# An attention and feed-forward block on one core: second batch in plain products, norm weights moved to the eviction, small work moved between engines

## The chip, the cores and the metric

The kernel runs on one core of one Trainium2 chip. The metric is the device time of one execution, in microseconds, from the first to the last instruction with what lies around them. The engines are TensorE (PE, with its weight loads PEld), VectorE (DVE), ScalarE (ACT), GpSimd (POOL) and SyncE (SP), whose queue issues all the transfers. TensorE's granted clock is given as a share of full speed: 1.00 is 2.4 GHz, and 0.50 is the lower of its two levels, 1.2 GHz.

## The reference, cut to what matters

Eight batches of 448 tokens, 12 heads of 64. Attention with normalised queries and keys, then a Fourier mix over tokens and channels, a layer norm, and a feed-forward with double precision weights that the kernel must first convert:

```python
rms = np.sqrt(np.mean(x * x, axis=-1, keepdims=True) + 1e-06)
q_n, k_n = (rmsnorm(q, g_q), rmsnorm(k, g_k))          # x / rms * g
scores = scale * np.matmul(q_n, k_n.transpose(0, 1, 3, 2))
attn = np.exp(scores - np.max(scores, axis=-1, keepdims=True))
x = np.matmul(attn / (attn.sum(axis=-1, keepdims=True) + 1e-09), v)
...
mixed = np.real(np.fft.fft(np.fft.fft(x, axis=1), axis=2))
u = x + mixed
un = (u - u.mean(-1, keepdims=True)) / np.sqrt(u.var(-1, keepdims=True) + 1e-06)
out = u + np.maximum(un @ w_ch1, 0.0) @ w_ch2
```

`g_q` and `g_k` are vectors of 64, one weight for each channel of a head. Every channel of a query meets the same channel of a key, so the kernel multiplies both weights (and the scale, negated) into one vector `gneg` and applies it to the keys alone.

## The kernel before, in words

**Batches and their two halves.** For each batch b there is an auxiliary part, `aux(b)` (attention, Fourier mix, layer norm), and a main part, `ffn(b)` (24 tiles `up` of 18 products, and 36 tiles `down` of 12). `aux(0)` runs first, with 14 steps of `aux(1)` mixed in after its attention. Then `ffn(b)` runs merged with `aux(b + 1)`: both are generators that yield a written cost after every step, and `merge` advances the side work until its cost reaches `RATIO` times that of the main work (0.49; `RATIO_FIRST`, 0.45, for `ffn(0)`). Side steps left over when the main work ends are issued behind it. The kernel asks for a schedule from a timeline model (`schedule_with_timeline_sim=True`), so that the order of the instructions on an engine need not be the written one. `LAG` and `PACE` bind some of them in place.

**Split and plain.** A product in full precision is made either from split operands (high parts and low parts of each value, multiplied in several fast passes, type fp32r) or plainly (type f32). A split needs a ScalarE copy of the high part and a VectorE subtraction for the low part (`sub`); plain operands need one ScalarE copy. `PLAIN_PAIRS` and `PLAIN_SCORES` say which pairs of heads are plain: in batch 0 all six in the value product, and all but the first two in the scores. Every later pair is split. `vhl` holds the split values, `QT` and `KD`/`KL` the transposed queries and keys, `T` and `R` the transposed probabilities, `P` the probabilities, `S` the scores, `mn` their minima.

**The norms.** `norm_pair` squares queries and keys (`sq`, one tile of 112 x 1024 called qkn in the profile), sums (`ss`), takes a power on GpSimd, multiplies the keys by `gneg` (`kf`, called raw<-raw,gneg) and multiplies both by the norms (qkn<-raw,ss, two tiles of 112 x 512). Squares and weight products run on GpSimd but for the first pair; the norm products run on GpSimd for pairs 2 to 8 (counted over batches), else on VectorE.

**The conversion of the weights.** The weights come as doubles. `convert` loads a tile (dblw<-w), and then ScalarE makes two prepared words (lines 702 and 703), VectorE does three bit operations (704, 708, 712), GpSimd adds the low bits (716), ScalarE copies the high part (717) and GpSimd subtracts it for the low part (718). There are 60 tiles: 24 of 768 columns and 36 of 512. 14 are made early, beside `aux(0)`; 46 are made when `ffn(0)` needs them. Later batches read the stored results.

**The Fourier mix.** `fold` makes sums and differences of the transposed attention output on VectorE (first eo<-xT, two additions), `spectral` multiplies by constant matrices (y, ab), `token_tile` adds and normalises, and `ffn_input` transposes for the feed-forward (un, unT). In batch 1 all three folds come after the last pair.

Line 113 of the profile is the wrapper that most VectorE, ScalarE and GpSimd instructions go through, so those are told apart by their tiles. On TensorE, L362 and L365 are scores (plain, split), L439, L443 and L473, L478 value products (plain, split), L898 `up` (h<-unT,w) and L919 `down` (o<-hs,w).

Of the kernel before, what the change touches and what calls it, by code (L numbers as in the profile page):

```python
# [11 lines left out]
F32 = mybir.dt.float32  # L12
# [3 lines left out]
AF = mybir.ActivationFunctionType  # L16
# [29 lines left out]
PLAIN_PAIRS = range(NPAIR)  # L46
PLAIN_SCORES = range(2, NPAIR)
# [42 lines left out]
def spectral_block(ctx, tc, q, k, v, g_q, g_k, w1, w2, d1, d2, out, nb=B):  # L90
# [90 lines left out]
    gneg = cpool.tile([C, D], F32, name="gneg")  # L181
    gtmp = cpool.tile([C, D], F32, name="gtmp")
# [4 lines left out]
    def load_gains():  # L187
        nc.sync.dma_start(gneg, g_q.rearrange("(o d) -> o d", o=1).broadcast_to([C, D]))
        nc.sync.dma_start(gtmp, g_k.rearrange("(o d) -> o d", o=1).broadcast_to([C, D]))
        V.scalar_tensor_tensor(  # L190
            out=gneg, in0=gneg, scalar=-(D**-0.5), in1=gtmp, op0=ALU.mult, op1=ALU.mult
        )
# [49 lines left out]
    def norm_pair(b, p):  # L242
# [5 lines left out]
        (G if nth else V).tensor_tensor(out=sq, in0=flat, in1=flat, op=ALU.mult)  # L248
# [6 lines left out]
        kf = flat[:, 8:]  # L255
        (G if nth else V).tensor_tensor(
            out=kf, in0=kf, in1=gneg[:, None, :].broadcast_to([C, 8, D]), op=ALU.mult
        )
        for i in range(2):
            (G if 2 <= nth < NPAIR * 3 // 2 else V).tensor_tensor(  # L260
                out=qk[:, i].rearrange("t c h d -> t h c d"),
                in0=raw[:, i],
                in1=ss[:, 8 * i : 8 * i + 8]
                .rearrange("t (h c) -> t h c", h=2)[:, :, :, None]
                .broadcast_to([C, 2, NC, D]),
                op=ALU.mult,
            )
# [4 lines left out]
        (G if b < EARLY else V).tensor_tensor(  # L272
# [16 lines left out]
    def transpose_pair(b, p):  # L289
# [8 lines left out]
        if plain_s(b, p):  # L298
            T = []
            for i, tag in enumerate(("QT", "KD")):  # L300
# [8 lines left out]
                A.copy(t, pt[:, :S])  # L309
# [7 lines left out]
        for i in range(2):  # L317
# [7 lines left out]
            if i == 0:  # L325
                A.copy(QT[lo, 0], src[lo])
                A.copy(QT[hi, 1], src[hi])
                sub(QT[hi, 0], src[lo], QT[lo, 0])
                sub(QT[lo, 1], src[hi], QT[hi, 1])
            else:  # L330
                for h, sl in enumerate((lo, hi)):
                    A.copy(KD[sl, h], src[sl])
                    sub(KL[sl, h], src[sl], KD[sl, h])
                A.copy(KD[hi, 0], KD[lo, 0].bitcast(F32))
                A.copy(KD[lo, 1], KD[hi, 1].bitcast(F32))
# [355 lines left out]
    def convert(src, bits, part, name):  # L691
# [26 lines left out]
        behind(nc.gpsimd.tensor_tensor(  # L718
# [287 lines left out]
```

## Time and profile before

| | |
|---|---|
| median of 3 runs | 2237.56 us (2234.73 to 2239.64) |
| the profiled execution, its own time | 2231.58 us |
| its span, first to last instruction | 2229.8 us |
| granted TensorE clock, mean | 0.968 |
| TensorE busy | 2107.0 us (94%) |
| VectorE busy | 1577.0 us (71%) |
| ScalarE busy | 1033.3 us (46%) |
| GpSimd busy | 542.3 us (24%) |

The busy shares are means over stages of very different kinds, and matmul instructions overlap, so a busy TensorE is not one at its peak. Two products that follow each other without a gap are told apart by the distance of their starts.

### The profile page before, as it was taken

To read this page: it belongs to the slowest core of one execution; us is meant where nothing else is said; L and a number is where in the kernel's file an instruction comes from. 1 tells how busy PE (TensorE), PEld (TensorE's weight loads), DVE (VectorE), ACT (ScalarE), POOL (GpSimd) and SP (SyncE) were. 2 spreads that over 40 slices of the span, in tenths; PEclk is the share of its full clock that TensorE was granted. 3 is DMA by queue.
4 is the path that set the end of the run, shared out by engine and by line. 5 is a ranking of instruction groups with operands and counts; after the bars stand their busy time and mean duration, and the time that the engine had idled before them with its cause. 6 is when DMAs were issued, how large, how long until landed. Compare 5 with 4: busy or idle time off the path is not lost.

```text
span 2229.8 us, 31302 instructions
## 1 busy us (share of the span) xinstructions
PE 2107.0 (94%) x11212; PEld 1855.7 (83%) x11212; DVE 1577.0 (71%) x2975; ACT 1033.3 (46%) x2242; POOL 542.3 (24%) x334
## 2 busy tenths in 40 slices
PE   7877988588999999999999999999999999999997
PEld 3336867477999999999999999999999999998997
DVE  6676899887688587866788587866787577763122
ACT  5756766554554355524554355524554355422100
POOL 6753566554121021211121021111211021000000
PEclk8888989799999999999999999999999999999999
DMA  5456555567655675557656675557555674539665
GB/s 171 150 162 203 189 190 193 201 235 244 200 175 174 197 221 167 176 178 224 188 171 183 201 214 165 177 177 230 185 169 179 205 212 159 178 135 289 214 211 137
DMA packets 298237, 425.32 MB, mean 191 GB/s; under 512 B 186545, under 2 KB 224418, under 8 KB 298082
## 3 DMA queue, kind: packets, MB, share of 16 engines
q1 hardware_dynamic: 298082, 423.32, 61.1%
q8 instruction: 89, 1.46, 0.3%
q14 instruction: 66, 0.54, 0.1%
HBM read 363.47 MB, written 65.27 MB: 192 GB/s over the span
## 4 chain that ended last, share of the span: by engine, by line
PE 79%; DVE 8%; DMA 4%; ACT 3%; issue 3%; POOL 2%; SPq 0%; DVEq 0%; POOLq 0%; ACTq 0%
PE h L898 28%; PE o L919 28%; PE S L365 5%; PE av L473 4%; PE pt L461 4%; DMA dblw<-w 2%; PE y L578 1%; PE qk L320 1%; PE av L439 1%; DMA w<-w 1%; POOL magw L716 1%; DVE eo L113 1%; PE oT L864 1%; DVE mn L113 1%; DVE magw L712 1%
## 5 line engine op out<-in xcount | busy, mean ns | idle before, releaser
L919 PE MATMUL o<-hs,w 128*128 128x448 f32 x3456 | 795.2, 372 | 14.9 <-POOL w L718 3.5
L898 PE MATMUL h<-unT,w 128*128 128x448 f32 x3456 | 787.0, 373 | 13.8 <-DVE xT L113 8.1
L898 PEld LDWEIGHTS h<-unT,w 128*128 128x128 f32 x3456 | 646.3, 191 | 68.1 <-issue 8.5
L919 PEld LDWEIGHTS o<-hs,w 128*128 128x128 f32 x3456 | 641.6, 190 | 72.7 <-POOL w L718 5.4
L113 ACT ACTIVATE P<-S,mn 112x448 f32<-112x448 f32 x384 | 243.0, 635 | 226.4 <-DVE mn L113 215.3
L113 DVE TENSOR_REDUCE mn<-S 112x1 f32<-112x448 f32 x384 | 232.3, 617 | 65.0 <-PE S L365 42.3
L113 POOL TENSOR_TENSOR qkn<-raw 112x1024 f32<-112x1024 f32 x47 | 89.7, 1909 | 720.2 <-PE qk L320 476.3
L113 ACT ACTIVATE hs<-h 128x448 fp32r<-128x448 f32 x192 | 104.4, 544 | 305.5 <-PE h L898 304.5
L113 DVE TENSOR_TENSOR acc<-o,acc 128x448 f32<-128x448 f32 x240 | 148.9, 621 | 105.4 <-PE o L919 103.8
L113 DVE SCALAR_TENSOR_TENSOR hs<-h,hs 128x448 fp32r<-128x448 f32 x192 | 119.3, 622 | 134.6 <-ACT hs L113 132.8
L113 ACT CAST T<-pt 128x448 fp32r<-128x448 f32 x252 | 132.7, 532 | 143.9 <-PE pt L461 137.7
L473 PE MATMUL av<-T,vhl 128*128 128x448 f32 x504 | 179.8, 390 | 8.8 <-DVE T L113 5.3
L113 DVE TENSOR_TENSOR T<-pt,T 128x448 fp32r<-128x448 f32 x252 | 154.8, 617 | 28.4 <-ACT T L113 26.8
L113 POOL TENSOR_TENSOR ss<-ss,nhalf 112x16 f32<-112x16 f32 x48 | 143.6, 2992 | 119.9 <-DVE ss L113 112.7
L461 PE MATMUL pt<-ident,P 112*128 112x112 f32 x1008 | 145.8, 264 | 4.5 <-ACT P L113 2.7
L365 PE MATMUL S<-KD,QT 128*112 128x448 f32 x352 | 139.4, 397 | 5.5 <-ACT KD L113 2.4
L461 PEld LDWEIGHTS pt<-ident,P 112*128 112x128 f32 x1008 | 122.6, 143 | 24.7 <-ACT P L113 3.1
L113 POOL TENSOR_TENSOR rstd<-st,nhalf 112x1 f32<-112x1 f32 (+2 forms) x32 | 19.1, 595 | 493.2 <-DVE st L113 493.2
L365 PE MATMUL S<-rounded,QT 128*112 128x448 f32 x352 | 131.8, 376 | 1.2 <-DVE rounded L113 1.2
L113 DVE TENSOR_SCALAR P<-P,sm 112x448 f32<-112x448 f32 x288 | 122.0, 463 | 3.9
L473 PEld LDWEIGHTS av<-T,vhl 128*128 128x128 f32 x504 | 96.1, 192 | 20.0 <-DVE T L113 7.4
L716 POOL TENSOR_TENSOR magw<-magw,dblw 128x512 uint32<-128x512 uint32 (+1 forms) x46 | 71.3, 1551 | 64.1 <-DVE magw L712 41.6
(127 smaller groups left out, 2580.8 us busy)
## 6 DMA issues: line engine op xcount, KB each, us to landing
w<-w SPq DMA_DIRECT2D x288, 512.0 KB, 4.4
w<-w SPq DMA_DIRECT2D x192, 768.0 KB, 4.5
dblw<-w SPq DMA_DIRECT2D x30, 512.0 KB, 4.4
dblw<-w SPq DMA_DIRECT2D x16, 768.0 KB, 4.5
raw<-q SPq DMA_DIRECT2D x96, 112.0 KB, 4.2
raw<-k SPq DMA_DIRECT2D x96, 112.0 KB, 3.8
v<-v SPq DMA_DIRECT2D x96, 96.0 KB, 3.6
u_dram<-u SPq DMA_DIRECT2D x24, 336.0 KB, 3.9
```

The costliest lines, as they stand in the source:

```text
L113: ins = emit(*args, **kwargs)
L320: nc.tensor.transpose(pt[:, c * C : (c + 1) * C], qk[:, i, c].rearrange("t h d -> t (h d)"), ident[:C, :C],)
L365: ins = nc.tensor.matmul(s_, QT[:, h, cs], K[:, h], start=step == 0, stop=step == 1)
L439: nc.tensor.matmul(av[:D, :S], vhl[:, j, h], T, start=j == 0, stop=False)
L461: nc.tensor.transpose(pt[:, c * C : (c + 1) * C], Pc[c][:, 512 * h + j * 128 : 512 * h + (j + 1) * 128], ident[:C, :C],)
L473: nc.tensor.matmul(av[:, :S], lv, T[:, i], start=(j == 0 and i == 0), stop=False)
L578: nc.tensor.matmul(o, src[:, par, t0 : t0 + n], D1[:, ri, par, cols], start=i != 1, stop=i != 0,)
L712: behind(nc.vector.scalar_tensor_tensor(out=bits, in0=high, scalar=0xC0000000, in1=bits, op0=ALU.bitwise_and, op1=ALU.bitwise_or,))
L716: behind(nc.gpsimd.tensor_tensor(out=bits, in0=bits, in1=low, op=ALU.add))
L864: nc.tensor.transpose(op[:n, j * 128 : (j + 1) * 128], accs[b][:, 3 * half + j, t0 : t0 + n], ident,)
L898: pace(nc.tensor.matmul(o, w[:, a, c], unT[c][:, z], start=n == 0, stop=n == 17))
L919: pace(nc.tensor.matmul(o, w[:, a, f], hs[4 * g + f][:, z], start=n == 0, stop=n == 11))
```

## The change

Batch 1 becomes plain as batch 0 is: `PLAIN_PAIRS` and `PLAIN_SCORES` reach to 12 pairs. The weights of the norms are no longer multiplied into the keys; `gains` holds both vectors with one channel a partition (twice, for the two heads), and `gneg` is now a per-partition scale in the eviction of the transposed keys, plain or split. The squares of batches 0 and 1 go from GpSimd (the first from VectorE) to ScalarE; those of later batches stay on GpSimd. The norm products, the low part of the split values and the low part of the converted weights (line 718) all go to VectorE.

```diff
-PLAIN_PAIRS = range(NPAIR)
-PLAIN_SCORES = range(2, NPAIR)
+PLAIN_PAIRS = range(2 * NPAIR)
+PLAIN_SCORES = range(2, 2 * NPAIR)
...
-    gneg = cpool.tile([C, D], F32, name="gneg")
-    gtmp = cpool.tile([C, D], F32, name="gtmp")
+    gains = cpool.tile([128, 2], F32, name="gains")
+    gneg = gains[:, :1]
...
     def load_gains():
-        nc.sync.dma_start(gneg, g_q.rearrange("(o d) -> o d", o=1).broadcast_to([C, D]))
-        nc.sync.dma_start(gtmp, g_k.rearrange("(o d) -> o d", o=1).broadcast_to([C, D]))
+        for i, g in enumerate((g_q, g_k)):
+            for h in range(2):
+                nc.sync.dma_start(
+                    gains[64 * h : 64 * h + 64, i : i + 1],
+                    g.rearrange("(d o) -> d o", o=1),
+                )
         V.scalar_tensor_tensor(
-            out=gneg, in0=gneg, scalar=-(D**-0.5), in1=gtmp, op0=ALU.mult, op1=ALU.mult
+            out=gneg, in0=gneg, scalar=-(D**-0.5), in1=gains[:, 1:], op0=ALU.mult,
+            op1=ALU.mult,
         )
...
-        (G if nth else V).tensor_tensor(out=sq, in0=flat, in1=flat, op=ALU.mult)
+        if b < EARLY:
+            A.activation(sq, flat, AF.Square)
+        else:
+            G.tensor_tensor(out=sq, in0=flat, in1=flat, op=ALU.mult)
...
-        kf = flat[:, 8:]
-        (G if nth else V).tensor_tensor(
-            out=kf, in0=kf, in1=gneg[:, None, :].broadcast_to([C, 8, D]), op=ALU.mult
-        )
         for i in range(2):
-            (G if 2 <= nth < NPAIR * 3 // 2 else V).tensor_tensor(
+            V.tensor_tensor(
                 out=qk[:, i].rearrange("t c h d -> t h c d"),
...
-        (G if b < EARLY else V).tensor_tensor(
+        V.tensor_tensor(
             out=vhl[:, :, 1:3], in0=vt, in1=vhl[:, :, ::3], op=ALU.subtract
         )
...
-                A.copy(t, pt[:, :S])
+                if i == 0:
+                    A.copy(t, pt[:, :S])
+                else:
+                    A.activation(t, pt[:, :S], AF.Copy, scale=gneg)
...
-                    A.copy(KD[sl, h], src[sl])
-                    sub(KL[sl, h], src[sl], KD[sl, h])
+                    A.activation(KD[sl, h], src[sl], AF.Copy, scale=gneg[sl])
+                    V.scalar_tensor_tensor(
+                        out=KL[sl, h], in0=src[sl], scalar=gneg[sl], in1=KD[sl, h],
+                        op0=ALU.mult, op1=ALU.subtract,
+                    )
...
-        behind(nc.gpsimd.tensor_tensor(
+        behind(nc.vector.tensor_tensor(
             out=part[1], in0=value, in1=part[0], op=ALU.subtract
         ))
```

## Rows read from the trace of the kernel before

**Rows 1.** Windows: length, then PE, PEld, DVE, ACT, POOL busy (instructions), TensorE clock, DMA.
```profile
152.00:196.00 44.00, 23.30 (x120) 19.57 (x120) 34.30 (x63) 23.50 (x48) 17.26 (x12) 0.71 0.47 142
196.00:543.00 347.00, 289.45 (x1417) 250.99 (x1418) 293.93 (x456) 211.33 (x412) 205.89 (x131) 0.89 0.64 212
543.00:2229.80 1686.80, 1670.69 (x9221) 1531.42 (x9219) 1147.76 (x2306) 701.67 (x1563) 216.80 (x123) 1.00 0.62 190
```

**Rows 2.** Groups by line, VectorE, 196 to 543 us: busy us, mean ns, idle before.
```profile
L704 DVE TENSOR_SCALAR magw<-magw 128x512 f32<-128x512 f32 x28 | 21.0, 750 | 8.3 <-ACT magw L702 8.2
L708 DVE TENSOR_SCALAR magw<-magw 128x512 uint32<-128x512 uint32 x29 | 23.5, 812 | 0.3
L712 DVE SCALAR_TENSOR_TENSOR magw<-dblw,magw 128x512 uint32<-128x512 uint32 x29 | 27.3, 940 | 0.4
L113 DVE TENSOR_TENSOR T<-pt,T 128x448 fp32r<-128x448 f32 x36 | 21.8, 615 | 1.3 <-ACT T L113 0.9
L113 DVE TENSOR_TENSOR qkn<-raw,ss 112x512 f32<-112x512 f32 x10 | 16.4, 1674 | 0.9 <-POOL ss L113 0.9
```

**Rows 3.** Groups by line, VectorE, 600 to 2000 us.
```profile
L113 DVE TENSOR_TENSOR qkn<-raw,ss 112x512 f32<-112x512 f32 x64 | 41.4, 686 | 3.3 <-POOL ss L113 3.0
L113 DVE TENSOR_TENSOR vhl<-v,vhl 128x512 fp32r<-128x512 f32 x34 | 23.4, 687 | 17.0 <-ACT vhl L113 13.7 <-DMA w<-w 2.9
```

**Rows 4.** Groups by line, GpSimd, 196 to 543 us.
```profile
L718 POOL TENSOR_TENSOR w<-magw,w 128x512 fp32r<-128x512 f32 x30 | 44.0, 1466 | 34.2 <-ACT w L717 34.2
L716 POOL TENSOR_TENSOR magw<-magw,dblw 128x512 uint32<-128x512 uint32 x29 | 38.9, 1340 | 36.9 <-DVE magw L712 26.8 <-ACT u L113 4.1 <-DVE sm L113 2.9
L716 POOL TENSOR_TENSOR magw<-magw,dblw 128x768 uint32<-128x768 uint32 x16 | 31.2, 1949 | 26.5 <-DVE magw L712 14.7 <-issue 8.6 <-ACT hs L113 2.1
L718 POOL TENSOR_TENSOR w<-magw,w 128x768 fp32r<-128x768 f32 x16 | 30.1, 1888 | 12.0 <-ACT w L717 12.0
```

**Rows 5.** Timeline, VectorE: start us, duration us, instruction.
```profile
368.61 0.43 DVE L708 TENSOR_SCALAR magw<-magw 128x512 uint32<-128x512 uint32 x1
369.67 0.68 DVE L712 SCALAR_TENSOR_TENSOR magw<-dblw,magw 128x512 uint32<-128x512 uint32 x1
373.80 3.17 DVE L708 TENSOR_SCALAR magw<-magw 128x512 uint32<-128x512 uint32 x1
```

**Rows 6.** Timeline, GpSimd, the same moment.
```profile
372.74 2.14 POOL L113 TENSOR_TENSOR qkn<-raw 112x1024 f32<-112x1024 f32 x1
375.39 1.28 POOL L718 TENSOR_TENSOR w<-magw,w 128x512 fp32r<-128x512 f32 x1
```

**Rows 7.** Timeline, TensorE: plain products of batch 0, split ones of batch 1.
```profile
93.15 0.96 PE L443 MATMUL av<-R,v 64*64 64x448 f32 x2
94.05 1.76 PE L362 MATMUL S<-KD,QT 64*112 64x448 f32 x8
...
221.03 0.37 PE L365 MATMUL S<-KD,QT 128*112 128x448 f32 x1
221.24 0.36 PE L365 MATMUL S<-rounded,QT 128*112 128x448 f32 x1
```

**Rows 8.** Timeline, VectorE: the first additions of a fold, batches 0 and 1.
```profile
153.43 6.04 DVE L113 TENSOR_TENSOR eo<-xT 128x449 f32<-128x449 f32 x2 [0.26 <-ACT xT L113]
...
449.05 1.15 DVE L113 TENSOR_TENSOR eo<-xT 128x449 f32<-128x449 f32 x2
```

**Rows 9.** Timeline, TensorE: stages' beginnings and ends.
```profile
150.99 0.96 PE L443 MATMUL av<-R,v 64*64 64x448 f32 x2
...
196.09 0.71 PE L898 MATMUL h<-unT,w 128*128 128x448 f32 x1 [0.28 <-DMA w<-w]
...
491.84 0.36 PE L365 MATMUL S<-KD,QT 128*112 128x448 f32 x1
...
541.24 2.18 PE L919 MATMUL o<-hs,w 128*128 128x448 f32 x10
543.26 3.82 PE L898 MATMUL h<-unT,w 128*128 128x448 f32 x18
```

## The prediction, made before the change was run

> **What bounds the kernel now.** I read the windows first: the stretch in which one engine is full, then those before it. After 543 us TensorE is busy 1670.69 of 1686.80 us at a granted clock of 1.00, while VectorE is busy two thirds of that time [rows 1]. Nothing that the change moves between VectorE, ScalarE and GpSimd can shorten that part: it is a block of about 1687 us of matrix work that only starts earlier or later. Everything that the change can win or lose lies ahead of it, in three stretches [rows 1]: the attention of batch 0, its transform and normalisation (152 to 196 us), and the feed-forward of batch 0, which runs beside the attention and the transform of batch 1 and beside 46 weight conversions (196 to 543 us). The third is the long one. TensorE is busy 289.45 of its 347 us, at a granted clock of 0.89, so it has both gaps and slow periods. At the full clock that work would be about 289.45 x 0.89 = 258 us, 74% of the stretch. VectorE is busy 293.93 us, 84.7% of the stretch; GpSimd 205.89 us; ScalarE 211.33 us.
>
> Next I read which VectorE groups fill that stretch. The split of the transposed probabilities (T) is work that only a split batch has [rows 2]. Three bit operations of the conversion (lines 704, 708, 712) and the norm products (qkn) take far longer than the same tiles elsewhere: 750, 812, 940 and 1674 ns [rows 2], against 0.43, 0.43 and 0.68 us in quiet spots [rows 5] and 686 ns after 600 us [rows 3]. The timeline shows why. One instruction of line 708 lasts 3.17 us instead of 0.43 [rows 5]; it starts during a square of 2.14 us on GpSimd and ends at 376.97 us, when GpSimd's narrow subtraction has ended at 376.67 [rows 6]. While GpSimd works on tiles, these VectorE instructions stand still.
>
> The Trainium skill ("SBUF — State Buffer", section "SBUF: two separate sides") says that VectorE and GpSimd share a pair of ports, which one instruction holds for its whole length while the other waits; the 3.17 us agrees with it. The same rule speaks against this change as well: an instruction with two SBUF inputs that moves to VectorE can now be held, and can hold GpSimd's. By the rule alone, if each of the 46 moved subtractions waited for one whole instruction of line 716 (38.9 + 31.2 = 70.1 us in all [rows 4]), the stretch would end at 401 us; the rows, worked out below, give 327. The rule is one more reason behind the last rival.
>
> **The change part by part, in the stretch from 196 to 543 us.**
>
> VectorE loses the splits of batch 1. T: 36 instructions at 615 ns, 21.8 us [rows 2]. By the code there are four more kinds of the same width, which I price at T's mean: 12 splits of the remainders, 12 additions of the two value halves, 8 query remainders (pairs 2 to 5; the first two pairs are done earlier) and 10 key remainders, 42 x 0.615 = 25.8 us. Together 47.6 us.
>
> VectorE gains line 718: 30 tiles of 512 columns and 16 of 768 [rows 4]. Before shows no such instruction on VectorE. The nearest row is the value split of the later batches, a subtraction of the same shape at 687 ns [rows 3]; by columns the wide one is 1.03 us. That gives 30 x 0.687 + 16 x 1.03 = 37.1 us. The dear end is what GpSimd needs for them, 44.0 + 30.1 = 74.1 us [rows 4]. I take the cheap end, since it is a VectorE row. Two norm products come over at 686 ns [rows 3], 1.4 us. Together 38.5 us.
>
> The holding falls. The excess over the quiet durations is 28 x (750 - 430) + 29 x (812 - 430) + 29 x (940 - 680) + 10 x (1674 - 686) ns = 9.0 + 11.1 + 7.5 + 9.9 = 37.5 us [rows 2, 3, 5]. Of GpSimd's 205.9 us [rows 1] line 716 stays with 38.9 + 31.2 = 70.1 us, a third [rows 4]; a few squares and copies stay too, so I take 45% of the holding as left. By the code 144 conversion and norm instructions were exposed to it, and 48 join them (x 1.33): 37.5 x 0.45 x 1.33 = 22.4 us. The relief is 15 us; its ends are 0 and 37.5.
>
> VectorE's sum is then 293.9 - 47.6 + 38.5 - 15 = 269.8 us. At the same share, 84.7%, the stretch would take 318 us: 29 us less by VectorE alone.
>
> ScalarE takes the squares of batches 0 and 1, and loses the second copies of queries, keys and remainders and the value copies. It has 347 - 211 = 136 us free here [rows 1], so I cost it at nothing. The norms' weights now ride in the key eviction: a copy becomes a copy with a scale and a subtraction becomes a scaled one of the same size, nothing. The products with the weights vanish from GpSimd in all batches; after 543 us that is cover under a full TensorE, so nothing there either.
>
> TensorE gains work. In the trace a plain product shows as two instructions (72 for the 36 value products of batch 0 by the code), and such a pair takes 0.90 us, from 93.15 to 94.05 [rows 7]. Split instructions follow each other every 0.21 us [rows 7]. A plain value pair has 8 products, 7.2 us; a split one has 14 instructions, 2.9 us. Six pairs of batch 1 make 6 x 4.3 = 26 us more. The scores come out even: four plain products in 1.7 us [rows 7] make 3.4 us for a pair's eight, and sixteen split ones take 16 x 0.21 = 3.4. TensorE's work in the stretch thus rises from 258 to 284 us at the full clock and passes VectorE's 269.8: VectorE was the tighter engine, TensorE will be. If the tighter one again gets 84.7% of the time, the stretch takes 284 / 0.847 = 335 us; but TensorE can hold 99% where nothing keeps it waiting [rows 1]. Between VectorE's 318 and this 335 I take the middle, 327 us: **20 us less**. The ends are 290 us, if TensorE is kept full, and 381, below.
>
> Start: four small loads of weights are issued where two were. The weights are now needed only at the first key eviction, but the multiplication that joins them still stands in VectorE's queue. The two things point opposite ways, and I take 0.
>
> Up to 196 us: the two first fold additions at 153 us took 6.04 us under GpSimd's work, and 1.15 us in a quieter place [rows 8]. They stand on the chain to the transform, so 4.9 us; with about 1 us for the shorter norm chain (squares and products no longer behind each other on GpSimd) I take 6. The ends are 0, if the moved subtractions come in between, and 15.
>
> **The order of the work.** The merge hands out the side work by its written costs. A plain value pair costs 420 + 2(3 x 1180 + 760) = 9,020 instead of 420 + 2(3 x 800 + 190) = 5,600, so the side work of batch 1 rises from 66,480 to 87,000. The feed-forward of batch 0 hands out 0.45 x 164,160 = 73,900, and 3,540 were handed out before it. So the last 14 steps (9,520), which are the whole transform and normalisation of batch 1, now come behind the last tile of the feed-forward, where before they were done ten steps ahead of its end. What is late next is the first product of the next feed-forward. Before, the first product of batch 1's feed-forward followed the last one of batch 0's at 543 us with no gap [rows 9]: the chain was hidden. Uncovered, it can be seen in batch 0: from the last value product at 151 us to the first product at 196 us [rows 9], 44 us, or 39 without the 4.9 us of holding. VectorE worked 34.3 us in it [rows 1], 29.4 without the holding, which the sum above already counts as 29.4 / 0.847 = 35 us. So the least cost is 4 us, and TensorE's idle time there, 44 - 23.3 = 21 us [rows 1], is the next bound; 44 is the worst. I take 12.
>
> Sum: -20 - 6 + 12 = -14 us. Against the profiled execution (2231.58 us, span 2229.8) that is 2217.6; the median of the runs stands 6.0 us above it, so **2224 us**.
>
> **Rivals.**
>
> *TensorE is kept full.* If conversion tiles and probabilities arrive in time, the stretch shrinks to TensorE's own work, 290 us with a little idle time: -57 - 6 + 12 = -51, 2187 us. For it: VectorE stands 8.3 us ahead of line 704 [rows 2], waiting for a chain that gets shorter. Against it: TensorE idles 58 us there now [rows 1], and no one wait accounts for it.
>
> *The transform is uncovered.* The 14 steps cost their 44 us in full: -20 - 6 + 44 = +18, 2256 us. For it: the written costs. Against it: score products of batch 2 were issued at 491 us [rows 9], ahead of their written place, so the order on the engines is not strictly the written one. It decides from 26 us on.
>
> *VectorE becomes the tighter bound, on the other side.* Line 718 needs the result of a ScalarE copy, for which GpSimd idled 34.2 us ahead of the narrow tiles alone [rows 4]. On GpSimd that idling held up nothing; on VectorE, scores, splits and sums stand behind it. If each moved instruction costs what it did on GpSimd (77.1 us in place of 38.5) and no relief comes, VectorE has 323 us and the stretch takes 381: +34 - 6 + 12 = +40, 2278 us. It decides from the mean price at which the whole change wins nothing: the stretch may then be 341 us, VectorE 288.8, which leaves 57.5 us for 48 instructions, 1.20 us each, against 0.80 in my sum.
>
> **How the numbers follow.** Forecast 0.53, with a range of its own from 2200 to 2240; TensorE kept full 0.17; transform uncovered 0.17; VectorE tighter 0.13. The range from 2178 to 2262 takes in the first three and leaves out the last and the far end of TensorE's. A change of 0.2% (4.5 us) is about what these runs can tell from none. Faster: 0.43 + 0.17 = 0.60; same 0.11, from the forecast's upper end and the mild form of the uncovered transform; slower 0.29, the rest of that form and the last rival.
>
> **What would show it.** After the change, in the stretch up to the second feed-forward: VectorE near 270 us; TensorE's busy time times its clock near 284 us; line 718 near 0.7 and 1.0 us; lines 704 and 708 nearer 0.43; the norm products nearer 0.69; the first fold additions near 1.2 us for two; a low TensorE clock with a gap between the feed-forwards of about 12 us more idle time. The forecast is wrong if the later block is not again about 1687 us, if line 718 is preceded by long VectorE waits, or if that gap is above 35 us.

## The result, and the profile after

The changed kernel takes 2201.66 us (median, 2199.90 to 2206.73) against 2238.60 us of the kernel before on the same chip: a ratio of 0.984, 95% interval 0.983 to 0.986, or 37 us less. The forecast was 14 us less. Its profiled execution lasted 2199.90 us with a span of 2198.1.

The windows of the changed kernel, cut at the first up product of each of the first two feed-forwards, answer to [rows 1] (length, then PE, PEld, DVE, ACT and POOL busy, TensorE clock, DMA):

```profile
0.00:185.00 185.00, 146.38 (x585) 73.66 (x585) 132.35 (x237) 127.51 (x275) 58.48 (x40) 0.87 0.55 167
185.00:504.00 319.00, 300.23 (x1384) 215.28 (x1385) 225.32 (x382) 181.65 (x354) 107.21 (x63) 0.98 0.70 228
504.00:2198.00 1694.00, 1674.88 (x9257) 1536.18 (x9256) 1164.38 (x2346) 723.06 (x1592) 179.15 (x93) 1.00 0.62 190
```

The first stretch is 11 us shorter (185 for 196), the second 28 us (319 for 347), the last block 7 us longer (1694 for 1687): the span falls by 32. The median fell 5 us more, since the profiled execution of before lay 7 us below its median and that of the changed kernel 2. In the second stretch VectorE's share fell from 85% to 71%, and TensorE's clock rose from 0.89 to 0.98. The same stretch in four parts shows what is left:

```profile
185.00:238.00 53.00, 53.00 (x233) 37.89 (x234) 18.26 (x33) 23.98 (x51) 8.77 (x6) 0.96 0.57 197
238.00:424.00 186.00, 179.00 (x810) 120.62 (x809) 145.02 (x233) 120.03 (x236) 73.35 (x43) 1.00 0.74 236
424.00:451.00 27.00, 19.00 (x80) 12.84 (x79) 24.97 (x36) 11.86 (x19) 8.62 (x5) 0.89 0.64 218
451.00:504.00 53.00, 49.24 (x267) 43.94 (x266) 37.07 (x82) 25.78 (x50) 16.47 (x11) 0.96 0.69 239
```

Up to 424 us TensorE is nearly full at the full clock. The one soft spot is 424 to 451 us, where the folds of batch 1 fill VectorE (24.97 of 27 us), TensorE is busy 19 us, and its clock is 0.89.

The VectorE groups of that stretch answer to [rows 2] (busy, mean ns, idle before; the lines are now 714, 718 and 722 for 704, 708 and 712, and 726, 727 and 728 for 716, 717 and 718):

```profile
L728 DVE TENSOR_TENSOR w<-magw,w 128x512 fp32r<-128x512 f32 x30 | 22.7, 759 | 12.1 <-ACT w L727 11.9
L722 DVE SCALAR_TENSOR_TENSOR magw<-dblw,magw 128x512 uint32<-128x512 uint32 x29 | 20.5, 707 | 0.3
L714 DVE TENSOR_SCALAR magw<-magw 128x512 f32<-128x512 f32 x28 | 17.0, 607 | 19.8 <-ACT magw L712 19.8
L728 DVE TENSOR_TENSOR w<-magw,w 128x768 fp32r<-128x768 f32 x16 | 16.7, 1042 | 2.1 <-ACT w L727 2.1
L718 DVE TENSOR_SCALAR magw<-magw 128x512 uint32<-128x512 uint32 x28 | 12.1, 432 | 0.5
L714 DVE TENSOR_SCALAR magw<-magw 128x768 f32<-128x768 f32 x16 | 11.6, 727 | 20.3 <-ACT magw L712 20.3
L113 DVE TENSOR_TENSOR qkn<-raw,ss 112x512 f32<-112x512 f32 x12 | 10.1, 871 | 0.7 <-POOL ss L113 0.7
```

The low part costs 759 and 1042 ns on VectorE, and the bit operations and norm products fell from 750, 812, 940 and 1674 ns [rows 2] to 607, 432, 707 and 871. On GpSimd the addition that stayed (line 726) has a longer mean than in [rows 4], 1540 ns for 1340. Twenty of the 29 still take 1.29 to 1.32 us. Six take 1.51 to 1.55 us and ran beside line 728 or a norm product; three take 2.0, 2.9 and 4.6 us, beside the folds and the transform of batch 1, and the longest of them met no subtraction of line 728.

```profile
L726 POOL TENSOR_TENSOR magw<-magw,dblw 128x512 uint32<-128x512 uint32 x29 | 44.7, 1540 | 91.7 <-DVE magw L722 51.6 <-ACT P L113 11.4 <-DMA v<-v 6.6
```

The timeline of VectorE at batch 0's last fold answers to [rows 8]; the two additions that took 6.04 us take 1.16:

```profile
140.88 1.16 DVE L113 TENSOR_TENSOR eo<-xT 128x449 f32<-128x449 f32 x2
142.07 1.17 DVE L113 TENSOR_TENSOR sd<-eo 128x450 f32<-128x450 f32 x2
```

And the timeline of TensorE where the two feed-forwards meet answers to [rows 9]:

```profile
498.21 2.27 PE L929 MATMUL o<-hs,w 128*128 128x448 f32 x10
500.32 1.15 PE L820 MATMUL un<-ident,un 112*128 112x112 f32 x10
502.29 0.60 PE L820 MATMUL un<-ident,un 112*128 112x112 f32 x4 [0.83 <-ACT un L113]
504.02 0.39 PE L908 MATMUL h<-unT,w 128*128 128x448 f32 x1
```

The last down product ends at 500.5 us, the first up product of batch 1 starts at 504.0, and most of the 3.5 us between is work. The transform of batch 1 ran beside the end of the feed-forward, ahead of its written place, as before.

### The profile page after: what moved, and what is told of

Same layout as the page of the kernel before. It is cut to its first block, busy times and chain, and to the rows that moved or that the text cites. A ratio compares the mean times of both kernels' runs of the same rounds, so it can differ in the third digit from the quotient of the medians.

```text
span 2198.1 us, 31240 instructions
## 1 busy us (share of the span) xinstructions
PE 2121.5 (97%) x11224; PEld 1825.1 (83%) x11224; DVE 1522.0 (69%) x2963; ACT 1032.2 (47%) x2218; POOL 344.8 (16%) x196
## 4 chain that ended last, share of the span: by engine, by line
PE 72%; DMA 2%; DVE 1%; ACT 0%; SPq 0%; issue 0%; DVEq 0%; ACTq 0%
PE h L908 27%; PE o L929 26%; PE S L375 5%; PE av L483 4%; PE pt L471 4%; PE y L588 1%; DMA w<-w 1%; PE qk L327 1%; PE oT L874 1%; PE av L488 1%; PE rem L430 1%; PE x L620 1%; PE ab L661 1%; PE un L820 1%; DMA u_dram<-u 0%; DVE u L113 0%
## 5 line engine op out<-in xcount | busy, mean ns | idle before, releaser
L908 PE MATMUL h<-unT,w 128*128 128x448 f32 x3456 | 773.9, 369 | 6.1 <-DMA w<-w 2.4
L113 POOL TENSOR_TENSOR qkn<-raw 112x1024 f32<-112x1024 f32 x36 | 69.2, 1923 | 692.7 <-PE qk L327 415.8
L113 ACT CAST T<-pt 128x448 fp32r<-128x448 f32 x216 | 113.0, 533 | 102.5 <-PE pt L471 100.9
L483 PE MATMUL av<-T,vhl 128*128 128x448 f32 x432 | 153.4, 383 | 0.0
L113 DVE TENSOR_TENSOR T<-pt,T 128x448 fp32r<-128x448 f32 x216 | 131.6, 618 | 27.5 <-ACT T L113 26.4
L375 PE MATMUL S<-KD,QT 128*112 128x448 f32 x304 | 119.3, 393 | 4.2 <-ACT KD L113 2.8
L471 PE MATMUL pt<-ident,P 112*128 112x112 f32 x864 | 121.4, 259 | 0.0
L471 PEld LDWEIGHTS pt<-ident,P 112*128 112x128 f32 x864 | 102.5, 140 | 15.6
L375 PE MATMUL S<-rounded,QT 128*112 128x448 f32 x304 | 113.4, 374 | 0.0
L483 PEld LDWEIGHTS av<-T,vhl 128*128 128x128 f32 x432 | 80.9, 188 | 7.2
```

What stands on the lines that cost most here:

```text
L113: ins = emit(*args, **kwargs)
L375: ins = nc.tensor.matmul(s_, QT[:, h, cs], K[:, h], start=step == 0, stop=step == 1)
L471: nc.tensor.transpose(pt[:, c * C : (c + 1) * C], Pc[c][:, 512 * h + j * 128 : 512 * h + (j + 1) * 128], ident[:C, :C],)
L483: nc.tensor.matmul(av[:, :S], lv, T[:, i], start=(j == 0 and i == 0), stop=False)
L908: pace(nc.tensor.matmul(o, w[:, a, c], unT[c][:, z], start=n == 0, stop=n == 17))
```

## The experiments

All runs are compared with the kernel before on their own chip. "Transform" is the start of batch 1's first Fourier product (y<-D) in the second stretch, "meeting" the first up product of batch 1; PE and DVE are busy time of the stretch, the clock TensorE's. All times in us, losses against the changed kernel by the medians.

| run | time | ratio [95%] | first up | transform | meeting | PE, clock | DVE | POOL |
|---|---|---|---|---|---|---|---|---|
| before | 2238.6 | 1 | 196 | 457 | 543 | 289, 0.89 | 294 | 206 |
| after | 2201.7 | 0.984 [0.983, 0.986] | 185 | 454 | 504 | 300, 0.98 | 225 | 107 |
| e1 low part on GpSimd | 2220.9 | 0.991 [0.990, 0.993] | 188 | 472 | 525 | 306, 0.95 | 231 | 176 |
| e2 batch 1 split | 2224.1 | 0.993 [0.991, 0.994] | 185 | 449 | 534 | 292, 0.88 | 293 | 110 |
| e3 norms on GpSimd | 2202.3 | 0.983 [0.982, 0.985] | 183 | 463 | 505 | 301, 0.97 | 229 | 115 |
| e4 ratio 0.55 | 2201.2 | 0.983 [0.981, 0.984] | 186 | 468 | 505 | 303, 0.98 | 235 | 103 |
| e8 plain scores, split values | 2213.9 | 0.989 [0.987, 0.991] | 183 | 433 | 522 | 296, 0.93 | 284 | 116 |
| e5 low part alone | 2237.0 | 1.000 [0.998, 1.001] | 196 | 452 | 546 | 293, 0.89 | 299 | 135 |
| e6 plain batch 1 alone | 2235.1 | 0.998 [0.997, 0.999] | 197 | 484 | 539 | 309, 0.95 | 236 | 192 |
| e7 norms alone | 2228.4 | 0.995 [0.993, 0.996] | 192 | 460 | 541 | 287, 0.90 | 291 | 182 |
| e11 weights alone | 2236.2 | 0.999 [0.998, 1.000] | 193 | 450 | 547 | 300, 0.88 | 289 | 195 |
| e9 idle tiles | 2232.3 | 0.998 [0.996, 0.999] | 197 | 508 | 537 | 313, 0.94 | 238 | 121 |
| e10 idle powers | 2216.4 | 0.990 [0.988, 0.992] | 191 | 478 | 517 | 307, 0.96 | 231 | 153 |
| e13 half of the values split | 2209.3 | 0.986 [0.983, 0.989] | 184 | 453 | 520 | 305, 0.94 | 264 | 104 |
| e14 plain values, split scores | 2222.9 | 0.993 [0.991, 0.996] | 184 | 493 | 524 | 303, 0.92 | 246 | 103 |
| e15 half of the scores split | 2218.1 | 0.992 [0.989, 0.995] | 185 | 493 | 520 | 303, 0.93 | 242 | 104 |
| e17 as e14, ratio 0.60 | 2199.2 | 0.983 [0.981, 0.985] | 184 | 420 | 505 | 297, 0.97 | 265 | 109 |
| e18 after, ratio 0.60 | 2200.4 | 0.983 [0.981, 0.985] | 184 | 451 | 503 | 302, 0.97 | 239 | 102 |
| e19 as e1, ratio 0.60 | 2224.8 | 0.993 [0.992, 0.995] | 186 | 464 | 533 | 323, 0.94 | 227 | 181 |
| e20 as e6, ratio 0.60 | 2230.9 | 0.996 [0.994, 0.997] | 196 | 444 | 544 | 321, 0.94 | 241 | 195 |

**One part undone in the changed kernel.** e1 puts the low part back on GpSimd, e2 splits batch 1 again, e3 puts the squares and norm products back on GpSimd, e4 hands the side work out earlier, e8 splits the values alone.

```diff
e1:
-        behind(nc.vector.tensor_tensor(
+        behind(nc.gpsimd.tensor_tensor(
             out=part[1], in0=value, in1=part[0], op=ALU.subtract
e2:
-PLAIN_PAIRS = range(2 * NPAIR)
-PLAIN_SCORES = range(2, 2 * NPAIR)
+PLAIN_PAIRS = range(NPAIR)
+PLAIN_SCORES = range(2, NPAIR)
e3:
-        if b < EARLY:
-            A.activation(sq, flat, AF.Square)
-        else:
-            G.tensor_tensor(out=sq, in0=flat, in1=flat, op=ALU.mult)
+        (G if nth else V).tensor_tensor(out=sq, in0=flat, in1=flat, op=ALU.mult)
...
-            V.tensor_tensor(
+            (G if 2 <= nth < NPAIR * 3 // 2 else V).tensor_tensor(
e4:
-RATIO_FIRST = 0.45
+RATIO_FIRST = 0.55
e8:
-PLAIN_PAIRS = range(2 * NPAIR)
+PLAIN_PAIRS = range(NPAIR)
```

> The changed kernel (2201.7 us) with one edit undone: the low part of the converted weights is subtracted on GpSimd again. Theory H (holding): GpSimd's tile work slows VectorE's conversion and norm instructions, so most of the gain goes: 2225 us or more, and lines 714 and 718 on VectorE are back near 0.75 and 0.8 us for 512 columns. Theory V (VectorE's sum): VectorE gets 39 us of work less in the stretch before the second feed-forward, so the time stays or falls: 2190 to 2202 us.

> The changed kernel with batch 1 split again in scores and values, all else kept. Theory V: VectorE gets back some 48 us of splits, from 229 to 277 us in the stretch, and the gain goes: 2230 us or more. Theory H: VectorE has room, 277 us at quiet durations, and TensorE is relieved of 26 us: 2195 to 2210 us.

> The changed kernel with the squares of the first two batches and the norm products of pairs 2 to 8 on GpSimd again. Theory H: 22 us more tile work on GpSimd before 185 us and some 12 us behind it: 8 to 15 us slower, with the first fold additions of batch 0 again above 3 us for two. Theory V: VectorE and ScalarE lose work: 0 to 5 us faster.

> The changed kernel with RATIO_FIRST 0.55 for 0.45, so that the merge hands out all of batch 1's side work (87,000 against 0.55 x 164,160 = 90,300) before the first feed-forward ends. Theory O (the written order costs): the transform's 14 steps are no longer behind the last tile, 8 to 15 us faster. Rival: the schedule had moved them ahead anyway: within 5 us of the changed kernel.

> The changed kernel with plain scores but split values in batch 1. TensorE is relieved of 26 us, VectorE gets the splits of T, R and the halves, 37 us, and of the values, 4 us: about 268 us. Theory B: VectorE binds again, at 84% 318 us for the stretch of 319: within 6 us of the changed kernel. If TensorE is what binds the changed kernel: 10 to 20 us faster. If VectorE's queue is the trouble: 10 us slower or more.

e1 loses 19 us, e2 22, e8 12; e3 and e4 lose nothing. The losses of e1 and e2 lie between their two theories, and e3 stays at the edge of its theory V; e4's rival and the last of e8's three cases came true. So the squares and norm products may run on either engine, and the written order, on which the forecast had put 12 us, decides nothing here. In e2 and e8 VectorE is back at 84% of the stretch with the durations quiet (in e2 the three narrow bit operations take 421, 478 and 737 ns): that with a split batch VectorE's own work sets the stretch is argued from this share, not shown (e17 below has 82% and loses nothing). In e1 it has only 69%, and the stretch is still 18 us longer; that needs another reason.

**One part alone on the kernel before.** e5 moves only the low part, e6 only makes batch 1 plain, e7 makes the three edits on the norms (weights, squares, products), e11 only puts the weights into the eviction.

```diff
e5:
-        behind(nc.gpsimd.tensor_tensor(
+        behind(nc.vector.tensor_tensor(
             out=part[1], in0=value, in1=part[0], op=ALU.subtract
e6:
-PLAIN_PAIRS = range(NPAIR)
-PLAIN_SCORES = range(2, NPAIR)
+PLAIN_PAIRS = range(2 * NPAIR)
+PLAIN_SCORES = range(2, 2 * NPAIR)
e7, e11:
-                A.copy(t, pt[:, :S])
+                if i == 0:
+                    A.copy(t, pt[:, :S])
+                else:
+                    A.activation(t, pt[:, :S], AF.Copy, scale=gneg)
...
e7 besides:
-        (G if nth else V).tensor_tensor(out=sq, in0=flat, in1=flat, op=ALU.mult)
+        if b < EARLY:
+            A.activation(sq, flat, AF.Square)
+        else:
+            G.tensor_tensor(out=sq, in0=flat, in1=flat, op=ALU.mult)
...
-            (G if 2 <= nth < NPAIR * 3 // 2 else V).tensor_tensor(
+            V.tensor_tensor(
```

> The kernel before (about 2239 us) with one edit: the low part of the converted weights on VectorE. Theory B (two bounds in a row: as long as batch 1 is split VectorE's sum binds the stretch, and only a plain batch 1 lets a shorter conversion chain count): VectorE stays near 290 us and the stretch near 347, so 2232 to 2240 us. Theory H (holding alone): the 16 to 18 us that this edit was worth in the changed kernel come here too: 2220 to 2224 us.

> The kernel before with one edit: batch 1 plain in scores and values. Theory B: VectorE falls to some 240 us and the stretch to about 337, as in the changed kernel with the low part on GpSimd; 2226 to 2231 us. Theory V (VectorE's sum alone): the stretch follows VectorE at 85%: 285 us, 2180 us.

> The kernel before with the norm edits alone: weights in the eviction, squares of the first two batches on ScalarE, products on VectorE; batch 1 split, low parts of weights and values on GpSimd. If the 11 us that the changed kernel wins ahead of the first feed-forward come from these edits: first product of the feed-forward near 186 us instead of 196, 2226 to 2231 us. If they come from the low part of the weights: first product at 192 us or later, 2234 to 2240 us.

> The kernel before with only the norms' weights moved into the key eviction: the products with the weights vanish, squares, norm products, low parts and value splits stay where they were. The run with all three edits on the norms began its feed-forward at 192.3 us instead of 196.1 and won 11 us; the changed kernel with squares and norm products back on GpSimd still won everything. If the weights are what counts among them: first up product at 191 to 193 us, time 2227 to 2231, 0.995 to 0.997. If the squares or the products' engine counts: first up product at 195 to 196 us and 2235 to 2239.

e5 came out by its theory B; e7 and e11 each met one of their cases by the first up product and the other by the time. Alone, the low part brings nothing (0.998 to 1.001), the plain batch 4 us, the norms 11, the weights 2. The sum of low part, plain batch and norms is 16 us, the whole change 37. Two together bring about their sum or a little more: plain batch and norms 19 us (e1), low part and norms 17 us (e2). The low part and the plain batch with the weights (and the value split on VectorE), but without the moved squares and norm products, bring all 37 (e3), though alone these three give 0, 4 and 2. So what the whole brings beyond the sum of its parts needs the low part and the plain batch together; the two without the weights were not run. In e5, e7 and e11 VectorE has 82 to 85% of the stretch, as before. In e6 it falls to 69%, and the stretch is 342 us all the same, and the time above both of its theories: with the low part on GpSimd a plain batch does not bring the end forward. In all five runs with the low part on GpSimd (before, e1, e6, e7, e11) the bit operations and norm products of the stretch take 35 to 48 us more than the quiet durations of [rows 3, 5]; in the six runs with it on VectorE (after, e2, e3, e4, e5, e8) 10 to 15. (This sum runs over both widths, the wide ones against 0.56, 0.56 and 0.95 us, which they take in quiet spots; e19, below, has 22.)

The start tells its own story. e11's timelines of VectorE and GpSimd show the holding on the same chain, one instruction later than in the kernel before; the two additions end when GpSimd's row of tile work has ended, at 156.54 us:

```profile
149.54 1.16 DVE L113 TENSOR_TENSOR eo<-xT 128x449 f32<-128x449 f32 x2 [0.26 <-ACT xT L113]
150.74 6.28 DVE L113 TENSOR_TENSOR sd<-eo 128x450 f32<-128x450 f32 x2
```

```profile
150.17 2.22 POOL L723 TENSOR_TENSOR magw1e<-magw1e,dblw1e 128x768 uint32<-128x768 uint32 x1
152.35 2.43 POOL L113 TENSOR_TENSOR qkn<-raw,ss 112x512 f32<-112x512 f32 x2
154.75 1.79 POOL L725 TENSOR_TENSOR w1e<-magw1e,w1e 128x768 fp32r<-128x768 f32 x1
```

Weights alone begin the feed-forward 3 us earlier, the low part alone at the same time; e3, which has both (and the value split on VectorE) but no moved squares or norm products, begins it 13 us earlier, and its folds are quiet.

**Idle work on GpSimd.** e9 and e10 add work that nothing reads, behind every addition of line 726.

```diff
e9:
+        behind(nc.gpsimd.tensor_tensor(out=idle, in0=idle, in1=idle, op=ALU.mult))    # 128 x 512
e10:
+        for _ in range(3):
+            behind(nc.gpsimd.tensor_tensor(out=idle, in0=idle, in1=nhalf[:, :1], op=ALU.pow))    # 128 x 1
```

> The changed kernel with one more multiplication of a 128 x 512 tile on GpSimd behind every addition of line 726 (work that nothing reads, added to the kernel). Putting the low part back on GpSimd cost 19 us in the run with that one edit undone. Theory H (holding): what costs there is that GpSimd works on tiles while VectorE wants to; then tiles that nobody waits for cost as well, 46 tiles of about 1.3 us, 60 us of GpSimd's time where the low parts were about 69: the stretch goes from 319 to about 332 to 336 us, the time to 2214 to 2220. Theory L (latency): what costs is that the converted tile comes out later; these tiles stand behind the addition that the conversion needs, so only the next tile's addition is later, and the time stays at 2200 to 2206.

> The changed kernel with three small powers of 128 x 1 numbers on GpSimd behind every addition of line 726 (work that nothing reads, added to the kernel). They take GpSimd's time with hardly any traffic on tiles. Theory H (holding of VectorE by tile work): no loss, 2200 to 2205 us, VectorE's durations as in the changed kernel. Theory L (GpSimd's queue makes the conversions late): if a power takes one to three us, GpSimd has 140 to 400 us more work, and the next addition is late: 2210 us or more. If both this and the run with more tiles stay at 2201, neither is the cause of what the low part costs on GpSimd, and only the place of the low part in the conversion's own chain is left.

They lost 31 and 15 us; 12 and 6 of these lie ahead of the first up product. e9 lost more than either theory gave it, and the two runs do not separate the theories, for a reason I had not seen: the schedule moved. Only 17 of the 60 idle tiles fell into the stretch, and nearly all of batch 1's transform went behind the last down product in e9 (it begins at 508 us, the last down product ends at 513, the meeting is at 537), and a part of it in e10. What e9 does show is a burst of eight idle tiles beside batch 0's last fold. GpSimd's and VectorE's timelines:

```profile
143.97 10.77 POOL L729 TENSOR_TENSOR idle<-idle 128x512 f32<-128x512 f32 x8
```

```profile
145.56 2.43 DVE L113 TENSOR_TENSOR eo<-xT 128x449 f32<-128x449 f32 x2 [0.26 <-ACT xT L113]
148.02 2.73 DVE L113 TENSOR_TENSOR sd<-eo 128x450 f32<-128x450 f32 x2
152.38 2.84 DVE L113 TENSOR_TENSOR eo<-sd 128x452 f32<-128x452 f32 x2
```

Each pair of additions took 2.4 to 2.8 us instead of 1.16: two engines taking turns. The Trainium skill ("SBUF — State Buffer", section "SBUF: two separate sides") calls the shared port pair an exclusive lock that the engine which starts first holds "for the whole instruction". That the two engines hold each other up agrees: the wait for each addition here was 0.6 to 0.8 us, and the eight idle tiles took 10.77 us, while one alone took 1.03 (the one at 141.19 us).

**Other divisions of batch 1.** e13 splits the values of its last three pairs, e14 the scores of all, e15 the scores of the last three pairs.

```diff
e13:
-PLAIN_PAIRS = range(2 * NPAIR)
+PLAIN_PAIRS = range(NPAIR * 3 // 2)
e14:
-PLAIN_SCORES = range(2, 2 * NPAIR)
+PLAIN_SCORES = range(2, NPAIR)
e15:
-PLAIN_SCORES = range(2, 2 * NPAIR)
+PLAIN_SCORES = range(2, NPAIR * 3 // 2)
```

> The changed kernel with the value products of the last three pairs of batch 1 split again (scores all plain). In the changed kernel TensorE fills its stretch (300 us busy of 319 at 0.98) and VectorE has 71%. Theory of two bounds: three split pairs take 3 x 4.3 = 13 us from TensorE and give VectorE half of the 60 us that the split batch costs, 255 us in all; at 84% that is 304 us, at TensorE's bound 306: stretch 304 to 312, time 2188 to 2196. Rival: VectorE binds before its share reaches 84%, since the split pairs stand in a row at the end of the batch: stretch 319 to 330, time 2201 to 2212.

> The changed kernel with split scores in batch 1, its values plain: the counterpart of the run with plain scores and split values. Between the all-split run and that one TensorE's busy time times its clock rose from 257 to 273 us, so plain scores seem to cost it 16 us, which the sum on record took as nothing; the remainders that come back cost VectorE 22 x 0.62 = 14 us. Theory A (TensorE's own work is the bound of the changed kernel's stretch): its work falls from 294 to 278 us, VectorE rises to 239 us, 79% of 303: stretch 301 to 308, time 2184 to 2193. Theory B (VectorE's load, above all around the transform, is the bound as well): stretch 319 to 330, time 2201 to 2213.

> The changed kernel with split scores in the last three pairs of batch 1 alone, values plain. Theory A (TensorE's own work is the bound): half of the former run's gain, TensorE 286 us, stretch 309 to 314, time 2191 to 2198. Theory B (VectorE's load is the bound as well, and the last pairs stand next to the transform): stretch 319 to 327, time 2201 to 2209.

e14 and e15 lost 21 and 16 us against the changed kernel. e13 lost 4 us by its ratio or 8 by its median, and its interval overlaps that of the changed kernel; at any rate it won none of the 5 to 13 us that the theory of two bounds gave it. That fits its rival: VectorE is busy 81 of the 84 us between 380 and 464 us, where the split pairs meet the folds. e14 and e15 fit neither theory, since neither engine is full (PE 303 of 340 us at 0.92, VectorE 246). The windows of e14, cut at the transform's start and the last down product's end, show the gap that the prediction had as a rival:

```profile
184.00:492.00 308.00, 276.12 (x1236) 208.01 (x1235) 226.05 (x354) 183.22 (x350) 100.53 (x60) 0.92 0.68 225
492.00:509.00 17.00, 17.00 (x109) 16.14 (x108) 10.38 (x19) 5.20 (x10) 1.31 (x1) 1.00 0.41 146
509.00:524.00 15.00, 10.32 (x54) 7.28 (x52) 9.87 (x33) 9.52 (x19) 1.28 (x3) 0.89 0.51 161
```

From 509 to 524 us TensorE has little but the transform's own work, 10 us busy, at a clock of 0.89.

**Handing the side work out earlier.** e17 is e14, e18 the changed kernel, e19 is e1 and e20 is e6, each with this:

```diff
-RATIO_FIRST = 0.45
+RATIO_FIRST = 0.6
```

> The run with plain values and split scores in batch 1 (2223 us), its side work handed out at 0.60 of the first feed-forward's cost instead of 0.45. Theory O (the written order put the transform behind the feed-forward): the transform starts before 470 us, the stretch comes to 301 to 315 us, the time to 2184 to 2200. Theory K (the chain of batch 1's attention with split scores is longer by itself: copies and subtractions between the transposes and the scores): the transform again starts after 480 us, the time stays at 2215 to 2226.

> The changed kernel with its side work handed out at 0.60 of the first feed-forward's cost instead of 0.45; at 0.55 nothing changed (2201). Theory O for the changed kernel (some of the transform's time at 450 to 504 us is still open and an earlier place hides it): 2190 to 2197. Theory K (its chain decides, not the written order): 2199 to 2205.

> The changed kernel with the low parts back on GpSimd (2221 us), its side work handed out at 0.60 of the first feed-forward's cost. Theory O (order): the transform starts by 455 us, the time falls to 2200 to 2208, and the low parts' engine is worth little. Theory H (holding: VectorE stands still while GpSimd works on tiles): the time stays at 2215 to 2223 wherever the transform starts, with the excess of VectorE's tile operations again near 35 us.

> The kernel before with plain batch 1 alone (2235 us), its side work handed out at 0.60. Theory O (order): the transform starts before 465 us and the time falls by 10 to 20 us, to 2215 to 2225. Theory H (holding by GpSimd's tile work, 173 us of it): 2230 to 2237.

e17 wins back some 23 us: its transform begins at 420 us, and e14's loss was the order of the work (e15 was not run so). It ends level with the changed kernel and not below it, and its stretch is 321 us where theory O had 301 to 315; VectorE has 265 of these, 82%. e18 changes nothing. e19 and e20 answer for the low part: with the transform early and done (un<-ident,un ends at 511 us in e19), the time stays within 5 us of where it was (4 more in e19, 4 less in e20). TensorE's timeline in e19 shows what is late instead, the feed-forward itself:

```profile
510.19 0.95 PE L820 MATMUL un<-ident,un 113*128 113x113 f32 x8
529.45 3.50 PE L929 MATMUL o<-hs,w 128*128 128x448 f32 x10
532.79 2.38 PE L908 MATMUL h<-unT,w 128*128 128x448 f32 x11
```

The feed-forward of batch 0 and the conversions go at one pace. The last low part of a weight tile ends at 528.6 us in e19 (on GpSimd) and at 497.3 in the changed kernel (on VectorE), and the last down product 4 and 3 us behind it:

```profile
527.36 1.27 POOL L728 TENSOR_TENSOR w<-magw,w 128x512 fp32r<-128x512 f32 x1 [3.51 <-ACT w L727]
```

```profile
496.62 0.68 DVE L728 TENSOR_TENSOR w<-magw,w 128x512 fp32r<-128x512 f32 x1
```

TensorE is hardly idle for it: it is busy 323 of e19's 347 us at a clock of 0.94, with some 10 us of work at the full clock more than in the changed kernel, since more of batch 2 comes in (50 score minima for 43). The last block is 7 us shorter for it. VectorE's lines in e19 show that the conversions come late (idle before, and what ended it; after had 19.8 and 20.3 us in these two groups):

```profile
L714 DVE TENSOR_SCALAR magw<-magw 128x512 f32<-128x512 f32 x29 | 14.9, 512 | 30.2 <-ACT magw L712 30.2
L714 DVE TENSOR_SCALAR magw<-magw 128x768 f32<-128x768 f32 x16 | 11.8, 735 | 29.3 <-ACT magw L712 29.3
```

and the waits of SyncE's queue over the stretch show why the loads are late: the load of the next raw tile (line 709) waits for GpSimd's addition of an older one (line 726), which reads that tile's buffer last. In e19:

```profile
SPq L709 <- POOL magw L726: 99.5, 39, 7.0
```

In the changed kernel:

```profile
SPq L709 <- POOL magw L726: 68.9, 32, 6.4
```

With the low part on GpSimd, the next addition stands behind a subtraction that itself waits for ScalarE's copy. In the plain versions with it there, that wait over the stretch is 93 to 109 us (e1, e6, e19, e20); with it on VectorE, 69 to 80 (after, e3, e4, e10, e13, e14, e18), but 86 in e17, which lost nothing, and 88 and 90 in e15 and e9. (With a split batch it is 89 to 102 even then, in e2, e5 and e8, where VectorE's own queue is full.) VectorE's holding explains the loss no better: its excess by the sum above is 22 us in e19, where theory H had 35, against 8 in e18, and e19 is 24 us slower; it is 35 in e1 against 11 in the changed kernel, and e1 is 19 us slower. That the queue of loads costs the 19 us, and not the holding, is argued from these rows; no run separated the two.

## Why the prediction was wrong, point by point

In the span the forecast was -14 us and the result -32. Of these 18 us the order of the work (step 3 below) made 12, the stretch (steps 1 and 2) 8 and the start (step 4) 5; the last block took 7 back. The median fell 5 us further than the span.

**Right.** The place: all of the gain lies ahead of the second feed-forward, and the later block is again full. VectorE was the tighter engine and is no longer. The splits that go were priced at 47.6 us; the same groups fell by 50 (T by 21.8, keys, queries, remainders and value halves by 28.5). The low part on VectorE was priced at 37.1 us and took 22.7 + 16.7 = 39.4. The first fold additions of 6.04 us fell to 1.16, as forecast. Plain batch 1 put TensorE's load up: its busy time by its clock rose from 258 to 294 us where I had 284. How that divides between values and scores stays open: plain scores (forecast as even) came out some 17 us dearer between e2 and e8, and only some 5 between e17 and the changed kernel.

**Step 1 that failed: "the relief is 15 us; its ends are 0 and 37.5".** I left 45% of the holding because line 716 keeps a third of GpSimd's time, and scaled it up for the instructions that join. By the same narrow groups the holding left is 28 x 177 + 28 x 2 + 29 x 27 + 12 x 185 ns = 8.0 us, not 22.4. The wide bit operations, which I had not counted, fell by 16 x (52 + 244 + 169) ns = 7.4 us more, and the fold's additions by 2.7. The relief was 37.5 - 8.0 + 7.4 + 2.7 = 39.6 us. Holding does not follow GpSimd's busy time: the changed kernel against e1 (11 for 35 us) and e5 against the kernel before (15 for 48) show that the low part on GpSimd carries 24 to 33 us of it (14 by e18 against e19), with the additions of line 726 there in all runs. Its move costs VectorE 39 us and gives most of that back.

**Step 2: "at the same share, 84.7%", and "between VectorE's 318 and this 335 I take the middle, 327".** VectorE's 225 us are 24 less than forecast by the holding, and some 20 less because work of batch 2 and the last transposes' additions slid behind the shorter stretch. At 84% that would be 268 us, so TensorE decides: 294 us of work in 319, full at 1.00 from 238 to 424 us. The stretch gave 28 us for 20; the rival that TensorE is kept full was nearest, at 17%, and the stretch went half of the 57 us that it gave. That the measured 319 us lies next to the 318 of "VectorE alone" is chance: VectorE had 225 us in it and not 269.8.

**Step 3: "I take 12" for the order of the work.** It cost nothing: the meeting has a gap of 3.5 us that is filled, and e4 and e18 hand the work out otherwise without effect. The 14 steps were counted from written costs, while the schedule follows a model of its own. But the mechanism is real: e14 paid some 23 us for it, and e9's transform stands in the same place (what it cost there was not tested). The rival was wrong for this kernel, not in kind.

**Step 4: up to 196 us, "I take 6".** It was 11. The fold gave its 4.9 us. Another 2 came at the very start, for which I had taken 0: the first transposes begin at 12.67 us for 14.68, and at 11.74 in e11, which moves the weights alone. The other 4 come from the chain between, for which no single row stands; that it runs quieter is not shown. e3 shows that the start needs no moved squares or norm products.

**Not foreseen:** the last block is 7 us longer, since the shorter stretch pulls less of batch 2 ahead (43 score minima in it for 51). The sum on record with the measured terms: -28 - 11 + 7 = -32 in the span.

## What to carry to other kernels

When several edits move work between engines, price the bound that each leaves behind: the low part alone brought nothing, the plain batch alone 4 us, and with the norms' 11 the whole brought 37, of which 19 or 22 were lost when the low part or the plain batch was undone. The likely reason is that another bound (VectorE's own work, or the pace of the conversions) stood close behind the first. Count what an instruction holds up on the neighbour engine from rows in which it is there and rows in which it isn't; its share of busy time does not tell. And where a planner orders the work, a small edit can move a whole chain behind its cover (23 us in e14), so look at where the chain starts before a loss is put down to the edit itself.

## What the runs showed of the hardware

A GpSimd power on 128 x 1 numbers took 0.62 us on average (180 of them, 112.2 us in e10), where one on 112 x 16 took 3.0; I had expected one to three. A subtraction that moved from GpSimd to VectorE fell from 1466 to 759 ns (512 columns) and from 1888 to 1042 (768), and the mean of the GpSimd addition that it left behind rose from 1340 to 1540 and from 1949 to 2080. Over the 29 and 16 tiles that rise is 8 us, while the bit operations and norm products on VectorE fell by 37.
